# A two-stage FFT filter and MLP kernel: batch 1's first stage moved behind batch 0's spectrum, x loads reordered, slots of the pairs moved

## The chip, the cores and the metric

One core of a Trainium2 chip. The time is device time of one execution in microseconds (us); the kernel before has a median of 544.36 us over 3 runs (544.21 to 546.55). Engines: TensorE (PE), VectorE (DVE), ScalarE (ACT), GpSimd (POOL) and SyncE (SP). SP and POOL also issue most of the DMAs; each of these queues runs in its order, and a DMA that waits holds what stands behind it in the queue.

## What is computed

```python
def _attn_ref(x, filt_r, filt_i):            # x: 8 x 3136 x 256
    X = np.fft.rfft(x, axis=1)
    F = (filt_r + 1j * filt_i)[None, :, :]
    y = np.fft.irfft(X * F, n=x.shape[1], axis=1)
...
def _moe_ref(x, U, V, w_ch1, w_ch2):         # x is the y of above
    h = x.transpose(0, 2, 1) @ U @ V
    u = x + h.transpose(0, 2, 1)
    ch = np.maximum(u @ w_ch1, 0.0) @ w_ch2
    return u + ch
```

Eight batches, each: a Fourier transform of length 3136 along the sequence, a product with a filter, the transform back, a low-rank mix along the sequence (rank 32), and a two-layer MLP with 1024 hidden channels and a residual.

## The kernel before

**The transform.** 3136 = 64 x 49. A first stage multiplies with the 64-point matrix w64; a second applies the 49-point transform with twiddles, one matrix per residue (t2, 32 of them); then the product with the filter (ft); then the inverse of the second stage (g12); then the inverse of the first stage, joined with the low-rank mix. The 32 residues go in 16 *pairs*. A pair of batches 1 to 7 in `stream` is: `forward` (L487, two matmuls, one PSUM bank of tag "x"), the product on VectorE (L495 for batch 1, L506 and L508 for later ones, with an add on POOL, L511), and two pairs later `i1` (L523, ScalarE copy L527).

**Layout changes go through DRAM for batches 1 to 7.** First stage `f1_units`: 13 units per batch, each one matmul (L449) and one copy (L453 or L455) into a staging buffer `asb` (two buffers); each of three x chunks is then written to c1 (L459, on SP for batch 1, on POOL for later ones). `load_a` (L468, SP) reads c1 back by residue in four groups; `i1` writes c2 (L529, SP), `load_e` (L475 and L480, SP) reads it into e2. `h1_unit` (L563, L568, L574, then four copies e<-e on SP) makes the low-rank part from the whole of e2.

**Batch 0 is the head** and stays on chip: `first_f1` (L348) into `at`; per pair `first_a` (four matmuls with the identity, L376, and a ScalarE copy, L378), `forward`, `both_products` (L495), `back` (L395, two copies L398); then 50 transposes into e2 (L432, copies L433), with `prep_u` between them; then `h1_unit(0)` and `make_u(0)` (L615, L621, L673). In `first_mid` one unit of batch 1's first stage (`next(fill)`) stands in each of pairs 7 to 15 and four stand between the L432. The tables t2 and g12 and the filters come in four parts (`PARTS`); `swap_real` and `swap_imag` copy a part of the filter to the other 64 partitions on VectorE.

**The loads** of the head all stand in POOL's queue: x of batch 0, first chunk; `load_rest` (odd filter rows); the other two chunks; then the four parts, with x of batch 1, first chunk, ahead of the fourth; then the rest of batch 1's x, U, V, w1 and w2. x tiles (tag "xt") have five buffers, shared with V.

**The MLP** goes in groups of four row pairs, 6 a batch and one of odd rows per two batches. Per group: eight `mm1` (two L680, copy with relu L688 on ScalarE, L686 on VectorE for a few), and in between `mm2` of the group before (L706 and L710, or, from batch 2 on, turned: L735, L739, L740). A group is eight *slots*; a batch 48 (SB). All work of later batches is put at slots by hand: `steps` gives the slot of every pair (batch 1 at 7.6 + 1.3k, batch 2 at 28 + 2.45k, later ones 3 apart from 18 on in the batch two before), `load_a` comes 9 to 14 slots ahead of its pairs, `load_e` some slots behind, `h1_unit` 9, 8 and 7 slots ahead of its batch, the units and x loads at slots of their own. The slots only set the order in which each engine and queue gets its instructions. The tile framework keeps this order (manual schedule).

Of the kernel before, what the change touches and what calls it, by code (L numbers as in the profile page):

```python
# [15 lines left out]
NS = 32  # L16
# [74 lines left out]
def kernel(  # L91
# [74 lines left out]

    w64 = cst.tile([128, 128], F16)
# [3 lines left out]
    t2 = cst.tile([98, NS * 128], F16)  # L171
# [51 lines left out]
    load_x(0, 0, ((0, 4), (4, 8)))  # L223
    load_rest()
    for c in range(1, len(CH)):
        load_x(0, c)
# [140 lines left out]
    def first_a(m):  # L367
        gi, ml = divmod(m, KG // 2)
        if ml == 0:
            st[0].setdefault("a", {})[gi] = sb.tile([98, KG * DM], F16, tag="a2", bufs=3, name="a2")  # L370
        pt = bank("o", "pt")
        for sl in range(2):
            for dh in range(2):
                o = sl * DM + dh * 128
                k = dh * 64 * NR + (2 * m + sl) * 98
                nc.tensor.matmul(pt[0:98, o:o + 128], at[:, k:k + 98], idn[:, :],  # L376
                                 start=True, stop=True, skip_group_check=True)
        nc.scalar.copy(st[0]["a"][gi][:, ml * 512:(ml + 1) * 512], pt[0:98, :])  # L378


    def first_mid(fill):

        et = sb.tile([128, 2 * NH * 128], F16, tag="e2", bufs=3, name="et")
        etv = et.rearrange("p (e r h k) -> p h e r k", e=2, h=2, k=64)
        pend = None

        def back(m, uv):
            pi = bank("fx"[m % 2], "pi")
            for sl in range(2):
                for dh in range(2):  # L390
                    for fi in range(2):
                        g = (4 * m + 2 * sl + fi) * 98
                        o = fi * 512 + sl * DM + dh * 128
                        a = (dh * 2 + sl) * 98
                        nc.tensor.matmul(pi[:, a:a + 98], uv[:, o:o + 128], g12[:, g:g + 98],  # L395
                                         start=(fi == 0), stop=(fi == 1), skip_group_check=True)
            for h in range(2):
                nc.scalar.copy(  # L398
                    etv[:, h, :, 0:NH - h, 4 * m:4 * m + 4],
                    pi[:, 0:392].rearrange("p (e k r) -> p e r k", e=2, r=NR)  # L400
                    [:, :, h * NH:h * NH + NH - h])

        def ahead(m):
            return forward(m, st[0]["a"][m // 4], ("m",))

        pxs = [ahead(0), ahead(1)]
        keep_on(8)
        for m in range(NS // 2):
# [4 lines left out]
            uv = both_products(m, pxs.pop(0))  # L413
            if pend is not None:
                back(*pend)
            pend = (m, uv)
            if m + 2 < NS // 2:
                pxs.append(ahead(m + 2))
            if m + 3 < NS // 2:
                first_a(m + 3)  # L420
            if m >= 7:
                next(fill)
        back(*pend)
        e2 = new_e2(0, 0)
        for k4, n0 in enumerate(range(0, NH, 4)):
            pt = ps.tile([128, 1024], F16, tag="m", bufs=BUFS["m"], name="pe")
            w = min(4, NH - n0)
            k = 64 if w == 1 else 128
            for rr in range(w):
                for dh in range(2):  # L430
                    o, a = rr * DM + dh * 128, (dh * NH + n0 + rr) * 128
                    nc.tensor.transpose(pt[0:k, o:o + 128], et[:, a:a + k], idn[:, :])  # L432
            (nc.scalar.copy if k4 in (1, 4, 6) else nc.vector.tensor_copy)(  # L433
                split(e2[0:k, n0 * DM:(n0 + w) * DM]), natural(pt[0:k, 0:w * DM]))
            if k4 == 1:
                prep_u()
            if k4 in (1, 2, 3, 4):
                next(fill)

    def f1_units(b, both):  # L440
        ne = 0
        for c in range(len(CH)):
            xt = st[b]["x"].pop(c)
            asb = sb.tile([128, 9 * DM], F16, tag="asb", bufs=2, name="asb")
            for n0 in range(0, CH[c], 2):
                w = min(2, CH[c] - n0) * DM
                k = 64 if c0[c] + n0 == NH - 1 else 128
                pf = bank("o" if b == 1 else "m", "pf")
# [3 lines left out]
                if both and ne % 2 and (b > 1 or ne >= 9):  # L452
# [29 lines left out]
    def forward(m, a2, xtags):  # L482
        ml = m % (KG // 2)
        px = bank(xtags[m % len(xtags)], "px")
        for sl in range(2):
# [28 lines left out]
    def stream():  # L514
# [26 lines left out]
        for p in pend:  # L541
            i1(*p)
            yield
# [101 lines left out]
    def make_u(gx):  # L645
# [6 lines left out]
        pms = [bank("m", "pu") for _ in range(2 if gx == 0 else 0)]  # L652
        for dh, pm in enumerate(pms):
            first_part(r0, nr, pm, 0, dh)
        if gx == 0:
            next(h1gen)
        for dh in range(2):
            if gx == 0:
                pm = pms[dh]
            else:  # L660
                pm = bank("m", "pu")
            if b:
                u_part(b, r0, nr, pm, 0, dh)
            else:
                if gx:
                    first_part(r0, nr, pm, 0, dh)
                first_low(r0, nr, pm, 0, dh)
# [4 lines left out]
            else:  # L672
                nc.scalar.copy(dst, pm)  # L673

    def mm1(gx, t):
# [9 lines left out]
        if t in ((4,) if b < TB or b == nb - 2 else () if b < nb - 1 else (1, 4, 6)):  # L685
# [4 lines left out]
    def mm2(gx, rr):  # L690
# [25 lines left out]
        if rr == nr - 1:  # L716
            for h in range(2):
                if nr == 1:
                    dst = rows(out, b - 1 + h, NR - 1, 1)
                else:  # L720
                    dst = rows(out, b, 2 * r0 + 4 * h, 4)
# [39 lines left out]
    NF = sum((c + 1) // 2 for c in CH)  # L761
    NP = NS // 2
    GP = NP // (NS // KG)
    SB = 48

    first_f1()
    swap_real(*PARTS[0])
    swap_imag(*PARTS[0])
    nc.vector.tensor_copy(ft[64:65, 0:DM], nyq[64:65, :])
    for m in range(3):  # L770
        first_a(m)
    vgen = v_order()
    for k, _ in enumerate(vgen):
        if k == 3:
            load_x(2, 0)
# [4 lines left out]
    first_mid(fill)  # L780
    h1gen = h1_unit(0)
    next(h1gen)
    make_u(0)
# [4 lines left out]
    steps += [steps[-1] + 3 * (k + 1) for k in range(LAG)]  # L788
    mid = stream()
    for k, t in enumerate(steps):  # L790
        put(t, mid)
        b, m = divmod(k - LAG, NP)
        if k >= LAG and m % GP == GP - 1:
            t += 6 if b > 1 else 4 if b else 2
            late = SB * b + 13
            if b and t < late:
                put(max(t, SB * b - 1), one(load_e, b + 1, m // GP, (0,)))
                put(late, one(load_e, b + 1, m // GP, (1,)))
            else:
                put(t, one(load_e, b + 1, m // GP))  # L800
    for b in range(1, nb):
        for gi in range(NS // KG):
            t = steps[NP * (b - 1) + GP * gi]
            put(max(0, t - (14 if b > 3 else 9 + b // 3)), one(load_a, b, gi))
        gen = h1_unit(b)
        for t in (9, 8, 7):
            put(SB * b - t, gen)
        if b > 1:
            fill = f1_units(b, b == 2)
            t0 = steps[NP * (b - 1)]  # L810
# [59 lines left out]
```

## Time and profile before

| what | value |
|---|---|
| median of 3 runs | 544.36 us |
| the profiled execution | 542.44 us |
| its span, first to last instruction | 540.7 us |
| mean granted TensorE clock | 0.986 |
| first L680 (MLP of batch 0 begins) | 61.05 us |
| last TensorE instruction starts | 534.16 us |
| DVE, ACT, POOL busy share | 75%, 69%, 53% |

The page divides the span into 40 slices (13.5 us each); a digit is the busy share in tenths. PEclk is the clock granted to TensorE in tenths, DMA the mean busy share of the 16 DMA engines. A group or timeline row names the line of the kernel, the engine, the operation, output<-input, a shape, and in brackets the idle time ahead of it and what ended that. The chain of work that ended last is followed back from the last instruction. In the head, the x loads of 256 KB took a median of 7.1 us from issue to landing, the parts of g 8.1 us, w1 12.4 and w2 14.4.

### The profile page before, as it was taken

To read this page: it belongs to the slowest core of one execution; us is meant where nothing else is said; L and a number is where in the kernel's file an instruction comes from. 1 tells how busy PE (TensorE), PEld (TensorE's weight loads), DVE (VectorE), ACT (ScalarE), POOL (GpSimd) and SP (SyncE) were. 2 spreads that over 40 slices of the span, in tenths; PEclk is the share of its full clock that TensorE was granted. 3 is DMA by queue.
4 is the path that set the end of the run, shared out by engine and by line. 5 is a ranking of instruction groups with operands and counts; after the bars stand their busy time and mean duration, and the time that the engine had idled before them with its cause. 6 is when DMAs were issued, how large, how long until landed. Compare 5 with 4: busy or idle time off the path is not lost.

```text
span 540.7 us, 11254 instructions
## 1 busy us (share of the span) xinstructions
PE 501.3 (93%) x4022; PEld 305.0 (56%) x4022; DVE 404.5 (75%) x582; ACT 374.3 (69%) x762; POOL 284.5 (53%) x402
## 2 busy tenths in 40 slices
PE   4775999999999999999999999999999989999995
PEld 3664567767667675555555555555555555444444
DVE  6885267777887668887888788888899878445663
ACT  2766766677668668877788778887777577655541
POOL 7676532336645536675676666855656564313000
PEclk9978899999999999999999999999999999999999
DMA  8999998967889587987899797987776755644333
GB/s 132 203 188 198 177 218 223 239 191 165 210 237 232 146 182 196 187 222 185 185 229 229 178 203 203 229 204 156 183 185 150 161 118 130 139 90 79 78 70 97
DMA packets 118346, 94.98 MB, mean 176 GB/s; under 512 B 52817, under 2 KB 100626, under 8 KB 118290
## 3 DMA queue, kind: packets, MB, share of 16 engines
q0 software_dynamic: 21984, 42.52, 38.8%
q1 hardware_dynamic: 96146, 51.43, 37.4%
q8 instruction: 31, 0.51, 0.4%
q10 hardware_dynamic: 160, 0.33, 0.3%
q14 instruction: 25, 0.20, 0.1%
HBM read 57.25 MB, written 48.17 MB: 195 GB/s over the span
## 4 chain that ended last, share of the span: by engine, by line
PE 72%; DVE 9%; DMA 9%; ACT 5%; issue 3%; POOL 2%; SPq 0%; DVEq 0%; ACTq 0%; POOLq 0%
PE phh L680 25%; PE po L735 20%; PE po L706 7%; PE px L487 5%; DVE uv L508 4%; PE pi L523 4%; DMA xt<-in_x_dram 4%; PE pu L606 3%; PE pf L449 3%; PE ph L563 2%; DMA e<-e 2%; ACT h L688 2%; DVE uv L506 2%; DMA g<-gd 1%; DMA c<-asb 1%
## 5 line engine op out<-in xcount | busy, mean ns | idle before, releaser
L688 ACT ACTIVATE h<-phh 128x512 f16<-128x512 f32 (+1 forms) x376 | 198.5, 577 | 79.0 <-PE phh L680 74.2
L680 PE MATMUL phh<-ut,w 128*128 128x512 f16 x768 | 197.7, 379 | 1.8 <-ACT h L688 0.6
L511 POOL TENSOR_TENSOR y<-uv 128x512 f16<-128x512 f16 x96 | 111.2, 1160 | 110.8 <-DVE uv L508 65.1
L735 PE MATMUL po<-h,w 128*128 128x512 f16 x560 | 143.8, 379 | 0.0
L508 DVE TENSOR_TENSOR uv<-px,ft 64x512 f16<-64x512 f32 x192 | 132.2, 688 | 2.6
L680 PEld LDWEIGHTS <-w 128*128 128x128 f16 x832 | 78.3, 98 | 79.5 <-issue 4.6
L748 POOL DMA_DIRECT2D out_dram<-och x120 | 70.0, 591 | 47.3 <-DVE och L740 44.4
L527 ACT CAST esb<-pi 98x512 f16<-98x512 f32 x112 | 65.7, 587 | 37.9 <-PE pi L523 34.4
L506 DVE TENSOR_TENSOR uv<-px,ft 128x512 f16<-128x512 f32 x96 | 64.8, 675 | 26.6 <-PE px L487 23.9
L735 PEld LDWEIGHTS <-w 128*128 128x128 f16 x560 | 52.0, 98 | 52.8
L739 DVE TENSOR_TENSOR tt<-po,ut 128x512 f32<-128x512 f32 x70 | 48.4, 692 | 40.7 <-PE po L735 30.1
L706 PE MATMUL po<-w,h 128*128 128x256 f16 x448 | 58.1, 273 | 0.0
L487 PE MATMUL px<-a,t 98*128 98x256 f16 x256 | 49.8, 276 | 7.0 <-DVE uv L508 4.7
L455 ACT CAST asb<-pf 128x512 f16<-128x512 f32 (+1 forms) x83 | 48.0, 579 | 9.6 <-PE pf L449 7.6
L740 DVE STREAM_TRANSPOSE och<-tt 128x512 f32<-128x512 f32 x70 | 49.8, 712 | 2.4
L706 PEld LDWEIGHTS <-h 128*128 128x128 f16 x448 | 42.6, 98 | 10.2 <-issue 0.9
L495 DVE TENSOR_TENSOR uv<-px,ft 128x1024 f16<-128x1024 f32 x32 | 38.4, 1221 | 11.7 <-PE px L487 11.3
L487 PEld LDWEIGHTS <-t 98*128 98x128 f16 x256 | 22.0, 99 | 35.5 <-DVE uv L508 17.3
L449 PE MATMUL pf<-xt,w 128*128 128x512 f16 (+1 forms) x91 | 34.9, 385 | 5.5 <-DMA xt<-in_x_dram 4.4
L670 ACT CAST ut<-pu 128x512 f16<-128x512 f32 x70 | 38.1, 609 | 0.0
L523 PE MATMUL pi<-y,g 128*98 128x256 f16 x192 | 36.7, 272 | 0.6 <-POOL y L511 0.6
L155 POOL DMA_DIRECT2D xt<-in_x_dram x50 | 30.4, 613 | 5.3 <-DMA xt<-in_x_dram 2.1
(91 smaller groups left out, 449.0 us busy)
## 6 DMA issues: line engine op xcount, KB each, us to landing
xt<-in_x_dram POOLq DMA_DIRECT2D x46, 256.0 KB, 6.7
a<-c SPq DMA_DIRECT2D x28, 392.0 KB
c<-esb SPq DMA_DIRECT2D x28, 392.0 KB
e<-c SPq DMA_DIRECT2D x56, 192.0 KB
out_dram<-och SPq DMA_DIRECT2D x160, 64.0 KB
c<-asb POOLq DMA_DIRECT2D x30, 256.0 KB, 4.6
out_dram<-och POOLq DMA_DIRECT2D x120, 64.0 KB, 3.2
out_dram<-och POOLq DMA_DIRECT2D x24, 256.0 KB, 5.0
```

The source lines that it names most:

```text
L449: nc.tensor.matmul(pf[:, 0:w], w64[:, :], xt[:, n0 * DM:n0 * DM + w], start=True, stop=True)
L487: nc.tensor.matmul(px[:, sl * DM:(sl + 1) * DM], t2[:, s * 128:(s + 1) * 128], a2[:, (2 * ml + sl) * DM:(2 * ml + sl + 1) * DM], start=Tru ...
L506: nc.vector.tensor_mul(uv[:, 0:512], px[:, :], ft[:, a:a + 512])
L508: nc.vector.tensor_mul(uv[p:p + 64, 512:1024], px[q:q + 64, :], ft[q:q + 64, b:b + 512])
L511: nc.gpsimd.tensor_add(y, uv[:, 0:512], uv[:, 512:1024])
L523: nc.tensor.matmul(pi[0:98, sl * DM:(sl + 1) * DM], g12[:, g:g + 98], y[:, o:o + DM], start=(fi == 0), stop=(fi == nf - 1), skip_group_che ...
L527: nc.scalar.copy(split(esb[:, ml * 512:(ml + 1) * 512]), natural(pi[0:98, :]))
L680: nc.tensor.matmul(pm[:, 0:w], w1[:, dh * 1024 + t * 128:dh * 1024 + (t + 1) * 128], ut[:, dh * w:(dh + 1) * w], start=(dh == 0), stop=(dh ...
L688: nc.scalar.activation(h[:, 0:w], pm[:, 0:w], RELU)
L706: nc.tensor.matmul(po[:, o:o + DM], hs[gx, t][:, rr * 128:(rr + 1) * 128], w2[:, t * DM:(t + 1) * DM], start=(t == 0), stop=False, skip_gr ...
L735: nc.tensor.matmul(po[:, :], w2[:, t * DM + dh * 128:t * DM + (dh + 1) * 128], hs[gx, t][:, :], start=(t == 0), stop=(t == 7))
L748: (nc.gpsimd if k and b < nb - 1 else nc.sync).dma_start(dst, och[32 * i:32 * i + 32, k * 512:(k + 1) * 512] .rearrange("p (r e) -> p r e" ...
```

## The change

- **Loads.** All of batch 0's x first, then `load_rest`; the first part of t2 on SP at the very start; batch 1's x behind the four parts, its three chunks spread over U, V, w1; batch 2's first chunk no longer within POOL's reordering of V.
- **Head.** `first_a` takes two pairs at a time, as transposes into one f16 bank with one copy. `forward` in the head gets eight small matmuls (`warm`) from pair 2 on. `keep_on(8)` goes. The first filter part is swapped in halves. Batch 1's units leave `first_mid`, but for four at its end; three stand in the new `first_u`, six in slots 0 to 3. `prep_u` and the clearing of e2 come earlier. `first_u` makes the first group's u, with its two copies on two engines.
- **Slots.** Batch 1's pairs at 12 + 1.25k, batch 2's at 41 + 2.2k, batch 3's at 76.5 + 2.45k, batch 4's at 115 + 2.8k; later ones two slots earlier than before and placed by position in the group (AT). Batch 1's `load_a` at slots 8, 11, 14, 19, its last pairs finished at once; `load_a`, `load_e`, `h1_unit`, first-stage units and x loads moved with them. x of batches 2 and 3 has new slots.
- **Small.** The relu copies of groups 0 and 1 go to VectorE four and three times instead of once; batch 6's one goes to ScalarE. The odd rows' output is one DMA instead of two.

```diff
+    t2 = cst.tile([98, NS * 128], F16)
+    nc.sync.dma_start(t2[:, 0:8 * 128], t2_d.ap()[:, 0:8 * 128])
...
     load_x(0, 0, ((0, 4), (4, 8)))
+    load_x(0, 1)
+    load_x(0, 2, ((16, 20), (20, 25)))
     load_rest()
-    for c in range(1, len(CH)):
-        load_x(0, c)
...
     for k, part in enumerate(PARTS):
-        if k == 3:
-            load_x(1, 0)
         if k:
             load_table(0, *part)
         load_filters(*part)
-        if k == 0:
-            load_table(0, *part)
         load_table(1, *part)
-    load_x(1, 1)
-    load_x(1, 2)
+    load_x(1, 0)
...
+    load_x(1, 1)
     w1 = cst.tile([128, 2 * 1024], F16)
...
+    load_x(1, 2)
     w2 = cst.tile([128, 8 * DM], F16)
...
     def first_a(m):
-        pt = bank("o", "pt")
-        for sl in range(2):
+        pt = ps.tile([128, 1024], F16, tag="o", bufs=BUFS["o"], name="pt")
+        for sl in range(4):
...
-                nc.tensor.matmul(pt[0:98, o:o + 128], at[:, k:k + 98], idn[:, :],
-                                 start=True, stop=True, skip_group_check=True)
-        nc.scalar.copy(st[0]["a"][gi][:, ml * 512:(ml + 1) * 512], pt[0:98, :])
+                nc.tensor.transpose(pt[0:98, o:o + 128], at[:, k:k + 98], idn[:, :])
+        for a, b in ((0, 512), (512, 1024)) if m == 0 else ((0, 1024),):
+            nc.scalar.copy(st[0]["a"][gi][:, ml * 1024 + a:ml * 1024 + b], pt[0:98, a:b])
+
+    def warm(px, n):
+        for k in range(8 * n):
+            o = k % 8 * 64
+            nc.tensor.matmul(px[:, o:o + 64], t2[:, 2 * o:2 * o + 128], t2[:, 0:64],
+                             start=True, stop=True, skip_group_check=True)
...
         def ahead(m):
-            return forward(m, st[0]["a"][m // 4], ("m",))
+            return forward(m, st[0]["a"][m // 4], ("m",), 0 if m < 2 else 1)
...
-        keep_on(8)
...
-            if m + 3 < NS // 2:
-                first_a(m + 3)
-            if m >= 7:
+            if m == NP - 2:
+                next(fill)
+            if m >= NP - 2:
                 next(fill)
+            if m % 2 == 0 and m + 4 < NP:
+                first_a(m // 2 + 2)
+            if m == 12:
+                e2 = new_e2(0, 0)
+        prep_u()
         back(*pend)
-        e2 = new_e2(0, 0)
+        next(fill)
...
-            if k4 == 1:
-                prep_u()
-            if k4 in (1, 2, 3, 4):
-                next(fill)
...
-                pf = bank("o" if b == 1 else "m", "pf")
+                pf = bank("oxof"[ne % 4] if b == 1 and ne > 3 else "m", "pf")
...
+    def first_u():
+        gen = h1_unit(0)
+        uts[0] = sb.tile([128, 1024], F16, tag="ut", bufs=3, name="ut")
+        next(gen)
+        pms = [bank("m", "pu") for _ in range(2)]
+        for dh, pm in enumerate(pms):
+            first_part(0, 4, pm, 0, dh)
+        next(gen)
+        for dh, pm in enumerate(pms):
+            first_low(0, 4, pm, 0, dh)
+            (nc.vector.tensor_copy if dh else nc.scalar.copy)(uts[0][:, dh * 512:(dh + 1) * 512], pm)
+        for k in range(3):
+            next(fill)
...
-        if t in ((4,) if b < TB or b == nb - 2 else () if b < nb - 1 else (1, 4, 6)):
+        if t in ((1, 3, 5, 7) if gx == 0 else (1, 4, 6) if gx == 1 else (4,) if b < TB else () if b < nb - 1 else (1, 4, 6)):
...
-    steps = [7.6 + 1.3 * k for k in range(NP)] + [28 + 2.45 * k for k in range(NP)]
-    for b in range(3, nb):
-        steps += [SB * (b - 2) + 18 + 3 * k for k in range(NP)]
+    AT = (0, 2, 5, 8, 10, 13, 16, 20)
+    steps = [[], [12 + 1.25 * k for k in range(NP + LAG)], [41 + 2.2 * k for k in range(NP)],
+             [76.5 + 2.45 * k for k in range(NP)], [115 + 2.8 * k for k in range(NP)]]
+    for b in range(5, nb):
+        steps.append([SB * (b - 2) + 16 + 24 * (k // 8) + AT[k % 8] for k in range(NP + LAG * (b == nb - 1))])
...
+            t = ends[GP * gi + GP - 1] + (6 if b > 2 else 3 if b > 1 else 2)
...
+    for t in (0, 0, 1, 1, 2, 3):
+        put(t, fill)
...
-            put(max(0, t - (14 if b > 3 else 9 + b // 3)), one(load_a, b, gi))
+            put((8, 11, 14, 19)[gi] if b == 1 else steps[b][GP * gi] - (14 if b > 3 else 2 * b + 2 - b // 3), one(load_a, b, gi))
...
-        for t in (9, 8, 7):
+        for t in (10, 9, 8) if b > 1 else (8, 7, 6):
             put(SB * b - t, gen)
...
-                put(4 + 1.1 * k if b == 2 else 18 + 2.8 * k if b == 3 else t0 - 54 + 3 * k, fill)
+                put(17 + 1.3 * k if b == 2 else 44 + 1.8 * k if b == 3 else t0 - 54 + 3 * k, fill2)
...
-    put(2, one(nc.sync.dma_start, low[0:64, :], low_d.ap()))
+    put(13, one(nc.sync.dma_start, low[0:64, :], low_d.ap()))
     for k in range(4):
-        put(1 + 2 * k, vgen)
+        put(4 + 2 * k, vgen)
```

More of the change, by code (lines that the diff above doesn't have):

```diff
@@ L122 @@
     BUFS = {"x": 1, "f": 1, "m": 4, "o": 2}
+    NF = sum((c + 1) // 2 for c in CH)
+    NP = NS // 2
+    GP = NP // (NS // KG)
+    SB = 48
     def bank(tag, name):
@@ L170 @@
     nc.sync.dma_start(idn, idn_d.ap())
-    t2 = cst.tile([98, NS * 128], F16)
     g12 = cst.tile([128, NS * 2 * 98], F16)
@@ L367, in first_a, with first_mid @@
     def first_a(m):
-        gi, ml = divmod(m, KG // 2)
+        gi, ml = divmod(m, 2)
         if ml == 0:
             st[0].setdefault("a", {})[gi] = sb.tile([98, KG * DM], F16, tag="a2", bufs=3, name="a2")
-        pt = bank("o", "pt")
-        for sl in range(2):
+        pt = ps.tile([128, 1024], F16, tag="o", bufs=BUFS["o"], name="pt")
+        for sl in range(4):
             for dh in range(2):
                 o = sl * DM + dh * 128
-                k = dh * 64 * NR + (2 * m + sl) * 98
-                nc.tensor.matmul(pt[0:98, o:o + 128], at[:, k:k + 98], idn[:, :],
-                                 start=True, stop=True, skip_group_check=True)
-        nc.scalar.copy(st[0]["a"][gi][:, ml * 512:(ml + 1) * 512], pt[0:98, :])
-    def first_mid(fill):
+                k = dh * 64 * NR + (4 * m + sl) * 98
+                nc.tensor.transpose(pt[0:98, o:o + 128], at[:, k:k + 98], idn[:, :])
[6 more added lines that the diff above has]
+                             start=True, stop=True, skip_group_check=True)
+    def first_mid():
         et = sb.tile([128, 2 * NH * 128], F16, tag="e2", bufs=3, name="et")
@@ L403, in ahead @@
         def ahead(m):
-            return forward(m, st[0]["a"][m // 4], ("m",))
+            return forward(m, st[0]["a"][m // 4], ("m",), 0 if m < 2 else 1)
+        first_a(1)
         pxs = [ahead(0), ahead(1)]
-        keep_on(8)
-        for m in range(NS // 2):
+        for m in range(NP):
             for k, part in enumerate(PARTS):
@@ L413, in first_mid @@
             uv = both_products(m, pxs.pop(0))
+            if m == 0:
+                swap_real(4, 8)
+                swap_imag(4, 8)
             if pend is not None:
@@ L416, in first_mid @@
             pend = (m, uv)
-            if m + 2 < NS // 2:
+            if m + 2 < NP:
                 pxs.append(ahead(m + 2))
-            if m + 3 < NS // 2:
-                first_a(m + 3)
-            if m >= 7:
+            if m == NP - 2:
                 next(fill)
+            if m >= NP - 2:
[5 more added lines that the diff above has]
+        prep_u()
         back(*pend)
-        e2 = new_e2(0, 0)
+        next(fill)
         for k4, n0 in enumerate(range(0, NH, 4)):
@@ L451, in f1_units @@
                 dst = asb[0:k, n0 * DM:n0 * DM + w]
-                if both and ne % 2 and (b > 1 or ne >= 9):
+                if both and ne % 2 and (b > 1 or ne > 3):
                     nc.vector.tensor_copy(dst, pf[0:k, 0:w])
@@ L480, in load_e, with forward @@
                 nc.sync.dma_start(e2[gi:64:4, 24 * DM:NH * DM], rows_[:, 24 * DM:NH * DM])
-    def forward(m, a2, xtags):
+    def forward(m, a2, xtags, n=0):
         ml = m % (KG // 2)
         px = bank(xtags[m % len(xtags)], "px")
+        warm(px, n)
         for sl in range(2):
@@ L540, in stream @@
                 yield
-        for p in pend:
-            i1(*p)
-            yield
+            if b in (1, nb - 1):
+                while pend:
+                    i1(*pend.pop(0))
+                    yield
     def one(load, *a):
@@ L651, in make_u @@
         uts[gx] = sb.tile([128, 1024], F16, tag="ut", bufs=3, name="ut")
[L652 to L656, printed above, removed]
         for dh in range(2):
[L658 to L661, printed above, removed]
+            pm = bank("m", "pu")
             if b:
@@ L664, in make_u @@
             else:
-                if gx:
-                    first_part(r0, nr, pm, 0, dh)
+                first_part(r0, nr, pm, 0, dh)
                 first_low(r0, nr, pm, 0, dh)
@@ L715, in mm2 @@
             nc.vector.tensor_copy(natural(och[:, a:(rr + 1) * DM]), split(po[:, 0:(rr + 1) * DM - a]))
-        if rr == nr - 1:
+        if rr == nr - 1 and nr == 1:
+            dst = bass.AP(tensor=out.tensor, offset=out.offset + ((b - 1) * SEQ + NR - 1) * DM,
+                          ap=[[SEQ * DM, 2], [RD, NQ], [1, DM]])
+            (nc.gpsimd if b < nb - 1 else nc.scalar).dma_start(dst, och[:, 0:DM])
+        elif rr == nr - 1:
             for h in range(2):
[L718 to L721, printed above, removed]
+                dst = rows(out, b, 2 * r0 + 4 * h, 4)
                 eng = nc.gpsimd if b < nb - 1 else nc.scalar if gx + 2 >= len(groups) and h else nc.sync
@@ L759, in run @@
             next(gen, None)
[L761 to L764, printed above, removed]
     first_f1()
-    swap_real(*PARTS[0])
-    swap_imag(*PARTS[0])
+    swap_real(0, 4)
+    swap_imag(0, 4)
     nc.vector.tensor_copy(ft[64:65, 0:DM], nyq[64:65, :])
-    for m in range(3):
-        first_a(m)
+    first_a(0)
     vgen = v_order()
-    for k, _ in enumerate(vgen):
-        if k == 3:
-            load_x(2, 0)
+    for _ in vgen:
+        pass
     for h in range(2):
@@ L779 @@
     vgen = u_units()
[L780 to L783, printed above, removed]
-    steps = [7.6 + 1.3 * k for k in range(NP)] + [28 + 2.45 * k for k in range(NP)]
-    for b in range(3, nb):
-        steps += [SB * (b - 2) + 18 + 3 * k for k in range(NP)]
-    steps += [steps[-1] + 3 * (k + 1) for k in range(LAG)]
-    mid = stream()
[L790 to L798, printed above, removed]
-            else:
-                put(t, one(load_e, b + 1, m // GP))
+    first_mid()
@@ new lines @@
+    first_u()
+    AT = (0, 2, 5, 8, 10, 13, 16, 20)
[3 more added lines that the diff above has]
+        steps.append([SB * (b - 2) + 16 + 24 * (k // 8) + AT[k % 8] for k in range(NP + LAG * (b == nb - 1))])
+    mid = stream()
+    for b in range(1, nb):
+        for t in steps[b]:
+            put(t, mid)
+        ends = (steps[b] + (steps[b + 1] if 1 < b < nb - 1 else []))[LAG:]
+        for gi in range(NS // KG):
+            t = ends[GP * gi + GP - 1] + (6 if b > 2 else 3 if b > 1 else 2)
+            late = SB * (b - 1) + 13
+            if b > 1 and t < late:
+                put(max(t, SB * (b - 1) - 1), one(load_e, b, gi, (0,)))
+                put(late, one(load_e, b, gi, (1,)))
+            else:
+                put(t, one(load_e, b, gi))
@@ L801 @@
+    for t in (0, 0, 1, 1, 2, 3):
+        put(t, fill)
     for b in range(1, nb):
+        t0 = steps[b][0]
         for gi in range(NS // KG):
-            t = steps[NP * (b - 1) + GP * gi]
-            put(max(0, t - (14 if b > 3 else 9 + b // 3)), one(load_a, b, gi))
+            put((8, 11, 14, 19)[gi] if b == 1 else steps[b][GP * gi] - (14 if b > 3 else 2 * b + 2 - b // 3), one(load_a, b, gi))
         gen = h1_unit(b)
-        for t in (9, 8, 7):
+        for t in (10, 9, 8) if b > 1 else (8, 7, 6):
@@ L807 @@
             put(SB * b - t, gen)
         if b > 1:
-            fill = f1_units(b, b == 2)
-            t0 = steps[NP * (b - 1)]
+            fill2 = f1_units(b, b == 2)
             for k in range(NF):
-                put(4 + 1.1 * k if b == 2 else 18 + 2.8 * k if b == 3 else t0 - 54 + 3 * k, fill)
+                put(17 + 1.3 * k if b == 2 else 44 + 1.8 * k if b == 3 else t0 - 54 + 3 * k, fill2)
             for c in range(len(CH)):
-                if b > 2 or c > 0:
-                    put(6 * c - 5 if b == 2 else 9 + 8 * c if b == 3 else t0 - 72 + 12 * c, one(load_x, b, c))
@@ L817 @@
-    put(2, one(nc.sync.dma_start, low[0:64, :], low_d.ap()))
+                put((0, 0, 9 + 4 * c, 36 + 6 * c, 52 + 11 * c)[b] if b < 5 else t0 - 72 + 12 * c,
+                    one(load_x, b, c))
+    put(13, one(nc.sync.dma_start, low[0:64, :], low_d.ap()))
     for k in range(4):
-        put(1 + 2 * k, vgen)
+        put(4 + 2 * k, vgen)
     slot = 0
```

## The prediction, before the result was known

> **What bounds the kernel now.** I read the share of busy time first, then the span in slices, then the chain of work and each engine's timeline over the head, and last the DMA queue's timeline where batch 0 hands over to batch 1. From the page, then the table of stretches (length; busy us and count of PE, PEld, DVE, ACT, POOL; PEclk; DMA share; GB/s):
>
> ```profile
> PE 501.3 (93%) x4022; PEld 305.0 (56%) x4022; DVE 404.5 (75%) x582; ACT 374.3 (69%) x762; POOL 284.5 (53%) x402
> PE   4775999999999999999999999999999989999995
> PEclk9978899999999999999999999999999999999999
> DMA  8999998967889587987899797987776755644333
> ```
> ```profile
> 20.00:40.00 20.00, 14.54 (x163) 12.03 (x161) 17.23 (x17) 12.56 (x35) 12.87 (x22) 0.83 1.12 191
> 40.00:60.00 20.00, 13.80 (x160) 10.27 (x156) 10.08 (x15) 11.96 (x30) 14.98 (x24) 0.83 1.02 192
> ```
>
> Two kernels in one: up to 61.05 us (the first L680, "t0" below) TensorE is idle a third of the time and the DMA share is about 1; from then on TensorE is nearly always busy. Its instructions from t0 on, counted in program order with the intervals of the timeline's rows (0.865 us for four L680, 0.875 for eight L706, 0.44 for four L523, 0.22 for two L487 ...), make 458.3 us; the last ends at 534.4, so only 15.1 us are idle in between (3.5 of them before 121). So a gain is to be had in the head, or in those 15 us. The chain of work in the head (start, us, what), and two waits of TensorE's timeline:
>
> ```profile
> 27.01 7.71 DMA xt<-in_x_dram
> ...
> 34.77 0.61 PE pf L449
> ...
> 41.52 6.90 DMA c<-asb
> ...
> 49.61 1.08 PE pe L432 x16
> ```
> ```profile
> 34.77 0.61 PE L449 MATMUL pf<-xt,w 128*128 128x512 f16 x1 [3.02 <-DMA xt<-in_x_dram]
> ...
> 49.61 1.07 PE L432 MATMUL pe<-idn,et 128*128 128x128 f16 x16 [2.77 <-ACT et L398]
> ```
>
> Both are batch 1's first stage standing in batch 0's way: L449 waits for x of batch 1, and the copy at 48.52 for a staging buffer still being written out.
>
> **The head, step by step.** (1) *x of batch 0.* load_rest leaves its way (0.22 MB), the first quarter of t2 takes its place on SP (0.2 MB): nothing; L348 ends at 16.7 as now. (2) *Start of the products.* One swap of two pairs instead of four stands ahead of the first L495 (0.75 us of DVE less), but the filters come 0.2 MB later: I take 19.4 for 19.91. (3) *The products.* VectorE paces them: 4.62 us for four, so 16 cost 18.5; the swaps still to come 0.75 + 3 x 1.4 = 4.9. End 42.8; now 46.1. Are the tables there? In bytes as they land, g's third part (4.7 MB down the queue) landed at 32.1 and x of batch 1, first chunk, at 34.7 (5.24 MB). At these 0.15 to 0.2 MB a us, with that chunk (3 us) taken out from ahead of them the last filters land near 35, wanted at 37; x's first chunk near 40, wanted at 41; w1 near 49, wanted at 52. (4) *first_a as transposes and warm.* The same 64 matmuls, and 14 x 8 of 64 columns: about 0.43 us a pair at 54 ns each, the interval of the 128-column ones; no row has the form, so between 0.2 and 0.9. TensorE's pair costs 0.84 now (L487 0.22, L376 0.22, L395 0.4), 1.27 then, under VectorE's 1.43 with swaps: nothing, as long as the clock stands. keep_on(8) goes: nothing, TensorE waits there. (5) *From the last product to L432.* 46.32 to 49.61 now, 2.0 of it for the staging buffer. Without that wait, with usb made ahead: 43.3 to 44.5. (6) *L432.* 8.0 us now with prep_u and four L449 between; 50 transposes alone, 2.7 us at the full interval (16 in 1.0), 5.3 at the half one (eight in 0.85): I take 4.5. (7) *To t0.* 57.6 to 61.05 now; the two copies of ut (1.07 in a row on ScalarE) go to two engines: 3.0. **t0 = 52.0, 9.1 earlier**; bounds 51 and 54.
>
> The Trainium skill bears on step 6 ("TensorE: Matmul & The Clock Gate", Part 4: PE-mode transpose): it says that a transpose does not count as work for the clock gate, so that the full rate does not engage for it. The trace agrees as far as it goes:
>
> ```profile
> 54.00:56.00 2.00, 2.00 (x18) 1.73 (x17) 1.41 (x3) 0.59 (x1) 2.00 (x5) 0.50 1.00 125
> ```
>
> TensorE is busy for all of that stretch, nearly all transposes, and granted half. Taken strictly, L432 would cost the 5.3 us and t0 would be 52.8.
>
> **After t0.** (8) Six of batch 1's 13 L449 move from the head into slots 0 to 3: 6 x 0.217 = **+1.3** of TensorE (459.5 in all). Nothing else is added: same counts of every L680, L706, L735, L487, L523. (9) Group 0 takes 10.25 us today for 8.3 of TensorE's work, with ScalarE busy without a break from 62 to 68; four of its eight relu copies (L688) go to VectorE, which sat idle for 6.1 us there: **-1.0** (0 to -2). w2 (landed 58.4, two copies of 1.0 on POOL) is wanted at t0 + 8.5 = 60.5: just there. (10) *New wait: batch 1's a.* Its last L449 stands 2.8 us of TensorE's work after t0, its first L487 11.2: 8.2 us (plus idle) for a copy (1.2), the write of c1 (SP waited for c<-asb 7 times, 26.1 us, so 3.7 each), and the load, which took at most 7.7 (issued 61.7, used 69.39). Its 392 KB alone are 2.0 at the 204 GB/s of 60 to 80 us. So 0 to 3.5; between 2.0 and 7.7 I take 4.5: **+0.5**. Behind a waiting L487 stands all of TensorE, in this step and the next two. (11) *New wait: e of batch 1.* Today the last L523 is at 108.77 and L563 at 121.23:
>
> ```profile
> 111.11 0.46 SPq L529 DMA_DIRECT2D c<-esb  x1
> 115.97 1.19 SPq L475 DMA_DIRECT2D e<-c  x2
> 117.21 0.58 SPq L480 DMA_DIRECT2D e<-c  x1
> ```
> ```profile
> SPq L475 <- DMA c<-esb: 46.3, 11, 7.8
> ```
>
> SP goes on as soon as it may, so these rows are the latency: 2.3 us to the issue of the write, 4.2 for the write (46.3 / 11; 3.6 to 8.2 in single cases), 1.8 to issue the reads, and at most 3.4 until L563, of which I take 2.4: 10.7. TensorE's work between the two is 12.0 us now and 8.2 then (slots 33 to 40). So L563 waits: 2.5 less some idle in between, **+2.0** (0 to 6). (12) *Batch 2 likewise*: 21.9 us of work now, 9.1 then: **+1.1** (0 to 5). From batch 3 on there are ten slots or more. h1 a slot earlier for the later batches costs nothing there; for batch 1 it is a slot later, and the e<-e that was 0.2 us late for the second group may be 0.9 late (within the range). (13) *Pairs closer together* (2.2, 2.45 and 2.8 slots a pair for batches 2 to 4, from 2.45 and 3): a product is 2.07 us of VectorE, and with a turned group's 2.8 it comes to 9.6 of 10 us in slots 96 to 113: **+0.5** (0 to 2). (14) *Place in the group* (from batch 5): L487 waits for VectorE are 3.1 us in all after 200; a third of it may go: **-1.0** (+1 to -3). (15) x of batch 2 behind batch 1's loads: chunks are due 8 to 10 slots after their slots; POOL is not held there, so nothing; low's load goes on SP from behind batch 1's first a to behind its second, wanted only at slot 44: nothing; one DMA for the odd rows in place of two: nothing, POOL waits for VectorE.
>
> **Sum.** -9.1 + 1.3 - 1.0 + 0.5 + 2.0 + 1.1 + 0.5 - 1.0 = **-5.7** against the profiled 542.44 (its span of 540.7 and 1.74 around it): 536.7. That execution stands 1.92 under the median of 544.36; against the median, **538.7**. The likeliest case's own range is 533 to 542.
>
> **The rivals.** *A: the hand-overs eat it.* For: with the longest write seen (8.2) and the full 3.4, step 11 costs 6 and step 12 some 5, and step 10 its 3.5: 11 more than taken, 550; half of that, 544.2. Against: those 8.2 us fell into a stretch with all three kinds of loads at once. 544.2, chance 0.16. *B: the head stays DMA-bound.* The share is 1 up to 60 us, and x1's third chunk, w1 and w2 lie only 0 to 3 us ahead of their use; were they 4 us later, TensorE would stand at t0 for as long: 542.7. Chance 0.08. This is also the case where the change does not do what it says, the order of the loads having no effect. *C, on the other side: the head's clock falls.* With transposes in place of L376, a pair would run at half rate; at 0.5 to 0.8 of the clock (27.73 to 31.14) pairs came every 1.7 us, and warm's 0.43 doubled makes 2.5. It decides where TensorE's pair passes VectorE's 1.43, that is under a clock of 0.9. Then 14 pairs cost 15 us more and t0 is near 67: 553.7; slower. Against: over two thirds of a pair's work stay ordinary matmuls, and from 18 to 26 us, with TensorE no busier than it will be, the clock kept 1.00. Chance 0.08. By the section of the Trainium skill named above this would come if too little ordinary work were left beside the transposes; no run here shows how much is too little.
>
> **Chances.** Forecast 0.68; A 0.16, B 0.08, C 0.08. A measurement tells 0.5% (2.7 us) from no change. Faster by more: 0.66 of the forecast, 0.01 of B: 0.67. Within: 0.02, 0.09 of A, 0.07 of B: 0.18. Slower: 0.07 of A, 0.08 of C: 0.15. Range: from 531 (t0 at 51, no new wait, all of steps 9 and 14) to 545 (A in the middle); left out are C, the worse part of A and a little below.
>
> **What would show it.** t0 at 51 to 54; no wait of L449's for x before L432; the clock at 1.0 from 20 to 43; L563 of batch 1 waiting 1 to 3 us for e<-c; idle after t0 of about 17 to 19 us. I am wrong if L487 of batch 1 or L563 wait for over 4 us, or if pairs in the head come slower than every 1.45 us.

## The result, and the profile after

**572.51 us median (566.98 to 580.45, 6 runs) against 544.4 (541.63 to 546.55, 6 runs): ratio 1.0503, interval 1.0461 to 1.0546. The change makes the kernel 5% slower.** Forecast were 538.7 and a gain; the result is outside the range and on the other side. Here and below, ratios leave out executions that fell in a slower state, here the one of 580.45.

The head did what was forecast: t0, the first L701 (L680 before), is at 52.59 instead of 61.05 (forecast 52.0). The rest lost far more than that. The page of the changed kernel, its span 572.0:

```profile
PE 513.5 (90%) x4126; PEld 307.1 (54%) x4126; DVE 405.3 (71%) x586; ACT 374.6 (66%) x753; POOL 284.3 (50%) x400
...
PE   5669499978989989789999999999999999999995
...
PEclk9999879988989979999999999999999999999999
DMA  8999957686868947997799869896895584545234
```

TensorE's row, before almost nothing but 9 from the fifth slice on, now has dips up to the 18th (slices are 14.3 us: 257 us), and PEclk dips beside them. The line numbers have moved: L701 is L680, L501 L487, L578 L563, L621 L606, L462 L449, L537 L523, L522 L508, L509 L495, L543 L529, L488 and L493 are L475 and L480, L481 is L468, L472 L459, L160 L155; L449 now stands for the transposes (L432). TensorE's timeline, the waits behind t0:

```profile
71.14 0.58 PE L501 MATMUL px<-a,t 98*128 98x256 f16 x2 [7.22 <-DMA a<-c]
...
123.03 0.79 PE L578 MATMUL ph<-e,ul 64*32 64x256 f16 x12 [2.92 <-DMA e<-c]
...
159.87 0.38 PE L501 MATMUL px<-a,t 98*128 98x256 f16 x2 [2.82 <-DMA a<-c]
...
201.15 0.51 PE L578 MATMUL ph<-e,ul 64*32 64x256 f16 x12 [1.89 <-DMA e<-c]
```

And two stretches from the table by time (length; busy us and count of PE, PEld, DVE, ACT, POOL; PEclk; DMA share; GB/s):

```profile
60.00:80.00 20.00, 12.78 (x75) 7.87 (x74) 5.61 (x7) 4.32 (x9) 0.00 (x0) 0.74 0.80 148
...
120.00:140.00 20.00, 14.60 (x124) 9.29 (x124) 8.28 (x12) 6.51 (x14) 5.34 (x7) 0.75 0.68 143
```

In the first TensorE is idle for 7.2 us, and the granted clock over the 20 us is 0.74: what runs behind the wait runs at about half rate. From t0 to the end of TensorE's last instruction it is 513.0 us, 473.4 before. Idle gaps take 35.3 of them (11.5 before): 12.7 for a, 5.8 for e, 13.9 for VectorE's products (5.5 before). Its work at full rate, by the prediction's count, is 459.5 (458.3). The rest, 18.2 (3.6), is put down to work slower than at full rate: **39.6 us lost = 23.8 of gaps + 14.6 of slower work + 1.3 of moved units**, up to rounding; 8.5 gained in the head. The difference, 31.1, is that of the two profiled spans (572.0 and 540.7) but for 0.2; between the medians it is 28.1.

The granted clock bears out the 14.6. Before, it is 1.00 over the whole of 61.05 to 534.40. In the changed kernel five stretches behind t0 have 0.50:

```profile
68.50:78.70 10.20, 7.55 (x33) 4.12 (x33) 3.05 (x3) 1.77 (x3) 0.00 (x0) 0.50 0.71 113
123.20:129.90 6.70, 6.14 (x64) 3.95 (x57) 0.71 (x2) 0.75 (x2) 0.00 (x0) 0.50 0.41 122
136.80:140.10 3.30, 3.30 (x14) 1.72 (x12) 2.07 (x3) 1.65 (x3) 0.43 (x1) 0.50 1.22 230
160.70:164.00 3.30, 3.30 (x26) 2.08 (x25) 2.42 (x4) 2.44 (x5) 1.15 (x1) 0.50 0.53 199
201.70:208.40 6.70, 6.27 (x53) 3.83 (x53) 1.38 (x2) 1.34 (x3) 1.78 (x3) 0.50 0.00 0
```

In them TensorE is busy for 26.6 us, of which half, 13.3, would have been saved at full rate.

The time from one batch's first L563/L578 to the next one's shows where, for these and for the kernels of the next section (us; each row is one profiled execution, which lies up to 4.6 us from its kernel's median):

| kernel | t0 | 0-1 | 1-2 | 2-3 | 3-4 | 4-5 | 5-6 | 6-7 |
|---|---|---|---|---|---|---|---|---|
| before | 61.1 | 63.6 | 64.7 | 61.5 | 57.5 | 59.9 | 56.0 | 54.2 |
| changed | 52.6 | 73.8 | 78.1 | 72.3 | 60.2 | 61.0 | 56.6 | 54.4 |
| e1, no x of batch 2 | 52.7 | 65.2 | 73.5 | 70.4 | 60.2 | 61.0 | 56.6 | 54.4 |
| e2, batch 1 late and fast | 53.3 | 67.9 | 82.8 | 70.9 | 60.2 | 61.0 | 56.6 | 54.4 |
| e3, warm in the wait | 52.1 | 71.5 | 75.4 | 69.5 | 60.2 | 61.0 | 56.6 | 54.4 |
| e4, longer lead | 53.0 | 75.2 | 75.1 | 68.4 | 60.2 | 61.0 | 56.6 | 54.4 |
| e5, x held | 52.0 | 68.4 | 72.1 | 72.1 | 60.1 | 61.0 | 56.6 | 54.4 |
| e6, both | 53.0 | 68.3 | 74.0 | 68.8 | 60.1 | 61.0 | 56.6 | 54.4 |
| e7, earlier end | 53.8 | 73.4 | 81.7 | 63.5 | 60.1 | 61.0 | 56.6 | 54.4 |
| e8, old slots | 54.6 | 72.2 | 64.8 | 61.2 | 57.4 | 59.9 | 56.0 | 53.0 |
| e9, e8 and batch 1 later | 54.6 | 71.9 | 64.7 | 61.1 | 57.5 | 59.9 | 56.0 | 52.9 |
| e10, e9 with units in slots | 52.5 | 81.0 | 65.0 | 61.1 | 57.4 | 59.9 | 56.0 | 53.0 |
| e11, e8 and new late places | 55.6 | 71.0 | 65.5 | 61.7 | 58.4 | 61.0 | 56.4 | 54.1 |
| e12, e8 and late batches 2, 3 | 57.6 | 70.0 | 68.7 | 68.0 | 57.4 | 59.9 | 56.0 | 53.0 |
| e13, e9 without x of batch 2 | 54.6 | 67.9 | 64.7 | 62.0 | 57.5 | 59.9 | 56.0 | 53.0 |

### The profile page after: what moved, and what is told of

It reads as the page before. It is cut to its first block, busy times and chain, and to the rows that moved or that the text cites. A ratio compares the mean times of both kernels' runs of the same rounds, so it can differ in the third digit from the quotient of the medians.

```text
span 572.0 us, 11457 instructions
## 1 busy us (share of the span) xinstructions
PE 513.5 (90%) x4126; PEld 307.1 (54%) x4126; DVE 405.3 (71%) x586; ACT 374.6 (66%) x753; POOL 284.3 (50%) x400
## 5 line engine op out<-in xcount | busy, mean ns | idle before, releaser
L701 PE MATMUL phh<-ut,w 128*128 128x512 f16 x768 | 200.3, 384 | 0.0
L522 DVE TENSOR_TENSOR uv<-px,ft 64x512 f16<-64x512 f32 x192 | 132.1, 688 | 2.6
L701 PEld LDWEIGHTS <-w 128*128 128x128 f16 x832 | 79.7, 99 | 79.0 <-issue 2.6
L770 POOL DMA_DIRECT2D out_dram<-och x120 | 70.8, 596 | 58.2 <-DVE och L762 51.9
L501 PE MATMUL px<-a,t 98*128 98x256 f16 x256 | 50.3, 278 | 27.8 <-DVE uv L522 13.3
L727 PE MATMUL po<-w,h 128*128 128x256 f16 x448 | 61.8, 284 | 0.0
L501 PEld LDWEIGHTS <-t 98*128 98x128 f16 x256 | 20.7, 99 | 58.5 <-DVE uv L522 28.9
L468 ACT CAST asb<-pf 128x512 f16<-128x512 f32 (+1 forms) x81 | 46.1, 575 | 8.5 <-PE pf L462 7.2
L727 PEld LDWEIGHTS <-h 128*128 128x128 f16 x448 | 44.1, 102 | 13.1 <-issue 3.5
L509 DVE TENSOR_TENSOR uv<-px,ft 128x1024 f16<-128x1024 f32 x32 | 38.2, 1220 | 16.1 <-PE px L501 15.2
L537 PE MATMUL pi<-y,g 128*98 128x256 f16 x192 | 37.0, 273 | 0.7 <-POOL y L525 0.7
L736 DVE COPY och<-po 128x512 f32<-128x512 f32 x26 | 18.0, 691 | 24.7 <-PE po L731 24.3
L745 POOL DMA_DIRECT2D out_dram<-och x24 | 13.0, 547 | 42.9 <-DVE och L736 42.9
```

The lines of the kernel that those rows point to most:

```text
L501: nc.tensor.matmul(px[:, sl * DM:(sl + 1) * DM], t2[:, s * 128:(s + 1) * 128], a2[:, (2 * ml + sl) * DM:(2 * ml + sl + 1) * DM], start=Tru ...
L522: nc.vector.tensor_mul(uv[p:p + 64, 512:1024], px[q:q + 64, :], ft[q:q + 64, b:b + 512])
L701: nc.tensor.matmul(pm[:, 0:w], w1[:, dh * 1024 + t * 128:dh * 1024 + (t + 1) * 128], ut[:, dh * w:(dh + 1) * w], start=(dh == 0), stop=(dh ...
L727: nc.tensor.matmul(po[:, o:o + DM], hs[gx, t][:, rr * 128:(rr + 1) * 128], w2[:, t * DM:(t + 1) * DM], start=(t == 0), stop=False, skip_gr ...
L770: (nc.gpsimd if k and b < nb - 1 else nc.sync).dma_start(dst, och[32 * i:32 * i + 32, k * 512:(k + 1) * 512] .rearrange("p (r e) -> p r e" ...
```

## Experiments

Theories: *contention* (x loads lie beside the transfers that TensorE waits for), *lead* or *room* (the new slots leave too little time for a chain of transfers), *clock* (each wait costs again in slow work), *late pairs* (VectorE cannot keep pairs so close). Ratios are to the kernel before.

**e1** (1.0362, 1.0302 to 1.0422; 562.74 us). Batch 2's x not loaded:

```diff
-            xt = st[b]["x"].pop(c)
+            xt = st[1 if b == 2 else b]["x"][c]
```

> Changed kernel without any load of batch 2's x: its first stage reads batch 1's x tiles instead (so batch 2's output is that of batch 1's x); every other instruction stays. In the changed kernel the four x DMAs of batch 2 issue at 57.2 to 59.6 us, just ahead of batch 1's a load (64.0), and L501 waits 7.2 us for it until 71.1. Theory 'contention' (those DMAs stretch the write of c1 and the load of a): the wait falls to 3 us or less, the half clock behind it goes too, total 6 to 10 us lower than the changed kernel. Theory 'lead' (write plus load take this long anyway, and the slots leave too little room): the wait stays at 5 us or more, total lower by under 4.

The first wait nearly goes. TensorE's timeline of e1, and POOL's of the changed kernel, where the four loads that collided stand; then SP's timelines, the changed kernel's and e1's:

```profile
65.11 0.38 PE L501 MATMUL px<-a,t 98*128 98x256 f16 x2 [1.06 <-DMA a<-c]
```
```profile
57.18 2.40 POOL L160 DMA_DIRECT2D xt<-in_x_dram  x4
```
```profile
55.03 2.87 SPq L472 DMA_DIRECT2D c<-asb  x4
64.03 0.92 SPq L481 DMA_DIRECT2D a<-c  x2
```
```profile
55.16 2.86 SPq L472 DMA_DIRECT2D c<-asb  x4
61.49 0.91 SPq L481 DMA_DIRECT2D a<-c  x2
```

The load of a waits for the write of c1. It is issued at 64.03 in the changed kernel and at 61.49 in e1, 6.1 and 3.5 us after the write's issues end; it lands 7.1 and 3.6 us later. Contention it is, for this wait; the one for e behind it grows from 2.92 to 3.96 us. The diff puts these loads at slots behind a's; but a slot only orders a queue, and POOL, with nothing in its queue that waits, issued them 7 us ahead of SP's load.

**e3** (1.0501, 1.0438 to 1.0564; 568.74 us). 192 `warm` matmuls ahead of the waiting L501.

> Changed kernel with 192 of the small warm matmuls put ahead of batch 1's first forward, where TensorE waits 7.2 us for a: some 5.6 us of work inside the wait. Theory 'clock' (a wait costs its length and then about as much again at half clock): the wait shrinks to 1 to 2 us, the first work behind it runs at full clock (four L701 in 0.87 instead of 1.7), total 3 to 4 us lower. Rival (the clock's loss is hidden by other waits): total the same within 1 us.

The stretch 60 to 80 of e3, and an L701 behind the wait, first in the changed kernel, then in e3:

```profile
60.00:80.00 20.00, 17.48 (x287) 14.01 (x285) 7.58 (x9) 5.97 (x12) 3.58 (x8) 1.00 0.85 154
```
```profile
76.02 1.91 PE L701 MATMUL phh<-ut,w 128*128 128x512 f16 x4
```
```profile
74.03 1.03 PE L701 MATMUL phh<-ut,w 128*128 128x512 f16 x4
```

Clock 1.00 instead of 0.74 with a still landing at 71.3, and the stretch 0-1 is 2.3 shorter, 1-2 2.7: that an idle TensorE brings the half rate is shown for this wait. The total's interval overlaps the changed kernel's, so 3 to 4 us off the total is not shown.

**e2** (1.0417, 1.0352 to 1.0483; 567.06 us): `[18 + 0.9 * k ...]` for `[12 + 1.25 * k ...]`.

> Changed kernel with batch 1's pairs at slots 18 + 0.9k instead of 12 + 1.25k: begun six slots later, ended at the same slot 33. Theory 'lead': the 7.2 us wait for a goes, with the half clock behind it (3 us): total 8 to 11 us lower, provided VectorE keeps up with pairs every 0.9 slots; the later waits for e stay. Theory 'contention': the load lands later again, wait of 3 us or more left.

The wait is 0.96, so room was a way out too. But only 5 us of total came. The profiled execution has later waits of 1.95 and 4.10 for batch 2's a; but it is the longest of the four (571.61), so they do not explain the median.

**e4** (1.0445, 1.0395 to 1.0494; 567.24 us): load_a of batches 2 and 3 (not the first) 11 slots ahead.

> Changed kernel with the loads of a for batches 2 and 3 (but the first of each) 11 slots ahead of their pairs instead of 6 and 7. Theory 'lead': the waits of L501 for a at 157 to 160 (2.8), 173 (0.4) and 234 to 237 (2.4) go, total 5 to 7 us lower. Rival (the load is held in SP's queue or by traffic, not by its slot): waits of 2 us stay, total the same within 1.5 us.

Those waits go, and stretches 1-2 and 2-3 are 3.0 and 3.9 shorter. Of the total, the medians differ by 5.3 us and the ratios by some 3; their intervals overlap.

**e5** (1.0336, 1.0273 to 1.0399; 562.47 us) and **e6** (1.0323, 1.026 to 1.0386; 561.24 us): x of batch 2 at `16 + c`, its first stage at `20 + 1.0 * k`; e6 has e4's edit as well.

> Changed kernel with all three x loads of batch 2 put at slots 16 to 18, so that they stand in POOL's queue behind the first group's output, which waits for VectorE (now they issue as soon as POOL is free, at 57 us); batch 2's first stage at 20 + 1.0k for 17 + 1.3k. Theory 'contention': as without those loads, L501 waits 1 to 2 us for batch 1's a instead of 7.2, batch 0's stretch (first L578 to batch 1's L578) falls from 73.8 to 66, total 562 to 565. Rival (the loads only collide with something else later: batch 1's later a loads, or c1 of batch 2): total over 568.

> The kernel with the x loads of batch 2 held, and batches 2 and 3's loads of a (but the first) 11 slots ahead. Theory 'waits add up': the 3 to 4 us that the longer lead gave alone come on top of the 8 to 10 of the held loads: 557 to 561. Rival (they are one and the same loss, each wait eating the next one's room): total as with the held loads alone, 562 to 565.

Held behind an instruction that waits, the loads do what the diff's slots meant: e5 is as good as e1. TensorE's timeline of e5:

```profile
64.27 0.38 PE L501 MATMUL px<-a,t 98*128 98x256 f16 x2 [0.36 <-DMA a<-c]
```

In e6 this wait is 1.42. From the end of the issues of c1's write to the landing of a it is 6.5 and 7.5 us in e5 and e6 and 7.1 in e1, against 13.2 in the changed kernel and 13.0 to 14.0 in e2, e3 and e4, where POOL issues x's four loads in the same place. But in both e5 and e6 L578 then waits for e, 6.91 and 6.38 us: the next link of the same chain. The gains do not add up: e6's total stands 1.2 us under e5's, with intervals that overlap, between what the two theories gave.

**e7** (1.0468, 1.04 to 1.0535; 568.32 us): e6 and

```diff
-[12 + 1.25 * k for k in range(NP + LAG)], [41 + 2.2 * k for k in range(NP)],
+[13 + 1.0 * k for k in range(NP + LAG)], [39 + 2.1 * k for k in range(NP)],
```

with batch 3 at 74 + 2.55k and batch 2's h1 at 9, 8, 7.

> The kernel with held loads and longer lead, and the pairs ended sooner ahead of the hand-over: batch 1 at 13 + 1.0k (last pair at slot 30 instead of 33), batch 2 at 39 + 2.1k (ended 3.4 slots earlier), batch 3 at 74 + 2.55k, batch 2's h1 a slot later. Theory 'too little room between c2 and h1': L578 of batch 1 and 2 no longer wait for e (4.0 and 2.2 us, with half clock behind each), 6 to 10 us lower than the kernel with held loads and longer lead: 549 to 554. Rival (VectorE, with pairs closer together, becomes the wait): L501 waits for VectorE by 5 us more, total within 3 us of that kernel.

L578 waits for e no more, as forecast, and stretch 2-3 falls to 63.5. But it is slower in all, by a wait that I had not looked for:

```profile
121.58 0.59 PE L501 MATMUL px<-a,t 98*128 98x256 f16 x2 [10.24 <-DMA a<-c]
```

A second one, of 7.25 us for batch 2's a as well, ends at 185.52. SP's timeline of e7 has the cause of the first: its queue stood at the read of e, which waited for c2's write, and a's load stands behind it.

```profile
104.36 0.93 SPq L543 DMA_DIRECT2D c<-esb  x1
113.62 1.19 SPq L488 DMA_DIRECT2D e<-c  x2
114.85 0.70 SPq L493 DMA_DIRECT2D e<-c  x1
115.79 1.01 SPq L481 DMA_DIRECT2D a<-c  x2
```

From the issue of that write to that of the read of e 9.3 us pass; the prediction reckoned with 4.2 for a write of c2.

**e8** (0.9934, 0.9904 to 0.9964; 540.49 us): the new head, all 13 units in it, and all the old slots and loads behind it. **This version beats both kernels, by 0.7% the one before.**

> Changed kernel's head and loads up to w2, with the slots of the kernel before for everything behind it (pairs, loads of a and e, h1, first stages and x of batches 2 to 7, low, V's order); all of batch 1's 13 first-stage units end in the head. Theory 'the slots lose it all': batches 1 to 7 take what they took before (64.7, 61.5, 57.5 ... between two L563), t0 is near 54, L501 waits 3 to 6 us for the first a, total 538 to 545. Rival (the new head itself causes the later losses, by the order of its loads): total above 550.

Stretches 1-2 to 6-7 are back to those of before within 0.3 (6-7: 1.2 less). So what the changed kernel loses behind batch 1's L578 is the slots' and the loads' that go with them. Ahead of it the old slots help less: from t0 to that L578 it is 60.2 us before, 67.0 in e8 and 70.4 in the changed kernel. In e8 L501 waits for the first a, landed 7.8 us after its issue at 60.76, and the clock is 0.50 from 65.7 to 72.5:

```profile
68.55 0.58 PE L501 MATMUL px<-a,t 98*128 98x256 f16 x2 [4.92 <-DMA a<-c]
```

**e9** (0.9945, 0.992 to 0.9969; 539.97 us) and **e10** (1.0089, 1.0061 to 1.0118; 548.33 us): e8 with batch 1's pairs at 12.5 + 0.95k; and with six units in slots 0 to 3 and 14 + 0.85k.

> The kernel with the new head and the old slots, batch 1's pairs at 12.5 + 0.95k instead of 7.6 + 1.3k (begun five slots later, ended at the same slot 27). Theory 'room': its wait of 4.9 us for the first a (landing 13.9 us after t0) and the half clock behind it go, so that the whole 6.4 us by which its head is shorter is kept: 534 to 537. Rival (pairs every 0.95 slots are too fast for VectorE and ScalarE): L501 and L537 wait for 3 us or more instead, 538 to 541.

> As that, but six of batch 1's first-stage units in slots 0 to 3 as in the changed kernel (t0 two us earlier, c1 later by as much against t0), and batch 1's pairs at 14 + 0.85k. Theory 'room': no wait for a over 1 us, the units cost the same there as in the head: 533 to 537. Rival: c1 comes too late and VectorE is too tight, 537 to 541.

Both theories miss. In e9 the wait for a is gone and nothing is gained; the total is the rival's, but L501 waits only 2.6 us for VectorE, in five waits, and L537 for nothing. Before, e8 and e9 reach batch 1's L563/L578 at 121.2, 121.7 and 121.3 us, with t0 at 61.1, 54.6 and 54.6. In e10, slower than either forecast, L462 waits 5.3 us for x (three times, 3.0 at most) and L537 3.0 for ScalarE.

**e13** (0.9911, 0.9884 to 0.9938; 538.49 us): e9 with e1's edit.

> The kernel with the new head, the old slots and batch 1's pairs at 12.5 + 0.95k, without any load of batch 2's x (its first stage reads batch 1's x tiles, so batch 2's output is that of batch 1's x). In the kernel with these loads, the one before it and the kernel before, batch 1's L563 all start at 121.2 to 121.7 us, though t0 is 54.6, 54.6 and 61.1. Theory 'bytes' (up to about 75 us the DMA engines are full, so what the head gains comes back as waits for the next data): without 1.6 MB of x, L563 starts 4 to 7 us sooner, total 533 to 536. Rival (VectorE and ScalarE set the pace of the first groups and of pairs 0.95 apart): L563 within 2 us of 121.3, total 538 to 540.

L578 of batch 1 starts at 117.33, 4.0 sooner than in e9, so data is at least part of what eats the head's gain; of the total only 1.5 us appear between the medians, less than the interval. What takes the rest stays open.

**e11** (1.0037, 1.0008 to 1.0066; 544.79 us) and **e12** (1.0109, 1.006 to 1.0158; 549.34 us): e8 with the changed kernel's places for batches 4 to 7; e8 with its late pairs for 2 and 3.

> The kernel with the new head and the old slots, but batch 4's pairs at 115 + 2.8k and those of batches 5 to 7 by place in the group (AT), as in the changed kernel. Theory 'the new places cost by themselves': the stretches between the later L563 grow from 57.4, 59.9, 56.0 and 53.0 to about 60, 61, 56.6 and 54.4, total 543 to 545. Rival (those stretches were longer in the changed kernel because its batch 3 came late): total 540 to 541 as without.

> The kernel with the new head and the old slots, but the pairs of batches 2 and 3 late and close together as in the changed kernel (41 + 2.2k and 76.5 + 2.45k, e and h1 of batch 2 with them); batch 1's first stage, its pairs, and all x loads and first stages of batches 2 and 3 stay early as in the kernel before. Theory 'late pairs alone': the stretches from batch 1's to 2's and 2's to 3's L563 grow from 64.8 and 61.2 to 68 or more each, by L563's wait for e of batch 2 and VectorE's pace: total 547 to 553. Rival (only the loads that collide with late pairs cost): both stretches within 1.5 us of 64.8 and 61.2, total 540 to 543.

Both cost by themselves, 4.3 and 8.9 us over e8, as the theories had it. L501's waits for VectorE from 300 to 460 us, first in e8, then in e11, where only the places differ (us, times, longest):

```profile
PE px L501 <- DVE uv L522: 2.1, 6, 0.5
```
```profile
PE px L501 <- DVE uv L522: 5.5, 12, 0.7
```

In e12 the waits in 205 to 231 are VectorE's:

```profile
212.21 0.39 PE L501 MATMUL px<-a,t 98*128 98x256 f16 x2 [0.71 <-DVE uv L522]
214.86 0.39 PE L501 MATMUL px<-a,t 98*128 98x256 f16 x2 [1.18 <-DVE uv L522]
...
228.00 0.39 PE L501 MATMUL px<-a,t 98*128 98x256 f16 x2 [1.19 <-DVE uv L522]
230.65 0.39 PE L501 MATMUL px<-a,t 98*128 98x256 f16 x2 [1.18 <-DVE uv L522]
```

The wait for batch 2's e that I expected there too did not come. Between the L578 of batches 1 and 3, L501's waits for VectorE (L522) are 6.3 us in e12 and 2.3 in e8; a further wait, 2.2, is for a. So VectorE is part of the 8.9, not shown to be all of it.

## Why the prediction was wrong, step by step

Ahead of t0 the sum had -9.1, and -8.5 came. Behind t0 it had +3.4 (steps 8 to 15), and 39.6 came.

- **Steps 1 to 7 (the head): the mechanism was right, the sum in part by luck.** t0 52.59 for 52.0. L462 no longer waits for x ahead of the transposes. They begin at 46.17, where step 5 had 44.5 at the latest, and from them to t0 it took 3.4 for 3.0; but 50 transposes took 3.08 (I took 4.5, between 2.7 and 5.3), which makes up for most of it. They ran at granted 1.00 (46.2 to 49.2), as did the matmuls ahead of them from 44.7 on; the Trainium skill's statement ("TensorE: Matmul & The Clock Gate", Part 4: PE-mode transpose) that the full rate does not engage for transposes, read strictly as step 6's 5.3, does not fit this run. Rival C did not come: the clock was 1.00 from 20 to 40.
- **Step 9 (-1.0) came.** What took 10.25 us from t0 before (to the sixth row of four L680) takes 8.43 now.
- **Step 15 (x of batch 2: nothing) failed first.** "POOL is not held there" is just why it cost: unheld, POOL put 1 MB of x beside the write of c1 and ahead of the load of a.
- **Step 10 (+0.5): 7.2.** Write 6 us for 3.7, load 7.1 for 4.5. Without the x loads it was 1.1, so the step would have been nearly right for a free path. The bound of 3.5 was no bound: I took 7.7 as the load's longest, but the write's mean. (The step's room is 11.2 - 2.8 = 8.4, not 8.2.)
- **Step 11 (+2.0): 3.5; step 12 (+1.1): 2.4.** Sizes off, mechanism right; with more room (e7) both waits are gone, though others come in their place.
- **Not in the sum: batches 2 and 3's a (5.5 us of waits)**, whose lead the diff cuts to 6 and 7 slots. I checked the hand-over c2 to e and not this one.
- **Not in the sum: the clock, 14.6 us, the largest single term.** The trace of before had it in the head: granted 0.50 from 34.3 to 37.6 us, around the end of the wait of 3.02, and from 51.4 to 58.1, behind the wait of 2.77. The sum priced every new wait at its length alone. e3 shows the link for the first wait. Not every wait brings the half rate: in e12 L501 waits 2.24 us up to 138.33, and the clock stays 1.00 from 130 to 150.
- **Step 13 (+0.5) and step 14 (-1.0).** L501's waits for VectorE grew from 5.5 to 13.9 us in all: those for L522 (L508 before) by 1.9 between the L578 of batches 1 and 3, and by 6.6 behind, where step 14 had forecast a gain. Alone, the places of batch 4 (step 13's) and of batches 5 to 7 (step 14's) cost 4.3 in total (e11); the late pairs of batches 2 and 3 cost 8.9, other waits included (e12). At the prediction's own 9.6 of 10 us, VectorE had hardly any room for unevenness.
- **Rival A named the right place**, with 550 at its worst; the clock and the waits for VectorE are what it lacked.
- **Where the head's gain goes with old slots** (e8, e9): 6.4 us at t0 come back as waits and slow work before batch 1's L578, which starts at 121.7 in e8 and at 121.2 before; for data at least in part (e13). What e8 gains in total, 3.3 us between the medians and 1.9 between the profiled spans, shows up behind that L578: 1.2 in the stretch 6-7 and 0.9 after it. Which of the small edits does this was not tested. Rival B did not come in its own form: no L701 or L727 of the changed kernel waits for w1 or w2, nor any L462 for batch 1's x.

## What to carry to other kernels

A slot in an order written by hand orders one queue; it holds nothing back on another. To put a load behind a transfer of another queue, stand it behind an instruction that waits. When a tuned pipeline is shifted later, follow every chain (write, load, pairs, write, read) through its queue at the longest latency seen, not the mean, and price each wait on TensorE with the slow work behind it.

## What the runs showed of the hardware beyond expectation

The same load of 392 KB (batch 1's first a) took 3.5 to 4.0 us from issue to landing with x's loads away (e1, e5, e6) and 7.1 to 10.5 beside them (the changed kernel, e2, e3, e4, e8). The waits for the write of c2 were 4.2 us on average before; in e7 one such write held the read behind it until 9.3 us after its issue. The wait of 7.2 us for a is followed by some 7 us of matmuls at half rate (four L701 in 1.7 us between starts, not 0.87), and 192 matmuls of 64 columns in that wait (e3) kept the full rate although TensorE still stood still for 1.2 and 0.9 us. Shorter waits did not all act alike: those of 2.92 and 2.82 us in the changed kernel had 6.7 and 3.3 us at granted 0.50 behind them, that of 2.24 in e12 none. What decides this no run here separates.
